# Attention heads whose transposed weights are spread over all 128 partitions by SBUF-to-SBUF transfers before their product with v

## The chip, the cores and the metric

The kernel runs on one core of a Trainium2 chip. Its engines are TensorE (PE, with its weight loads as PEld), VectorE (DVE), ScalarE (ACT), GpSimd (POOL), and SyncE (SP), whose queue issues all of this kernel's DMA transfers. The metric is the device time of one execution in microseconds. Span means the time from the first to the last instruction of the profiled execution.

## The reference

Two attention blocks over the same x (2048 tokens, 1024 wide, 32 heads of 32) are mixed by a gate per token. Block A is linear attention with a feature map phi, block B softmax attention:

```python
g = _sigmoid((x * gate_w).sum(-1, keepdims=True))
# A
pq, pk = phi(q), phi(k)
kv = jnp.einsum("bhsd,bhse->bhde", pk, v);  z = jnp.einsum("bhsd->bhd", pk)
o = jnp.einsum("bhqd,bhde->bhqe", pq, kv) / (jnp.einsum("bhqd,bhd->bhq", pq, z)[..., None] + 1e-6)
# B
scores = jnp.einsum("bhqd,bhkd->bhqk", q, k) * (Dh ** -0.5)
o = jnp.einsum("bhqk,bhkd->bhqd", softmax(scores), v)
# both: q, k, v are columns of x @ wqkv; o is brought to [2048, 1024] and multiplied by wo
return g * a + (1 - g) * b
```

All is float32. The kernel keeps that precision in its big products by splitting an operand into a high and a low part and adding three products (`three`).

## The kernel before

**Stages.** First, block B's v for the first 512 columns and all of its q and k are computed and stored to HBM (`v`, `qk`, and a second copy of v in another layout, `vh`). Then eight of B's heads (`NB = 8`) go one way (`bheads`), and the other 24 go another (`maxima` and `heads_`). The linear work of block A and the rest of v (`linear`, three matmuls L161 to L163 for each of eight k-steps, 512 columns each) fills TensorE beside both. The output projection comes last (`output`).

**The first eight heads.** They are worked on in 32 bursts, n = 4 h + J: head h and a quarter J of its 2048 query rows, that is four strips i of 128 queries. For each strip, four score matmuls (j, 512 keys each, L979) have 128 queries as rows. VectorE takes the maximum of each row in each block (L985, stored negated), ScalarE takes the exponential with that maximum as bias and the row sum beside it (L992, into a slot of `big20`), and VectorE transposes the 128 x 512 block in squares of 32 x 32 (L995, `move`). Since only squares are transposed, partition group a (32 partitions each) then holds, for its own 32 queries, keys m x 32 .. m x 32 + 31 of every square m. So in each group a key lies on 32 partitions only, and the product with v (`burst`, L865) is made of 32 x 32 x 128 matmuls: 16 squares m, four key blocks c, four groups a, 256 in a burst, with v copied to each of the four groups (`load_bv`, from `vh`). Four banks take the four groups' sums; the four key blocks c stand on different 32 rows of a bank, and each has been scaled by its own block maximum. ScalarE moves the four banks to `big2` (L871). At the end of a head `weigh` makes the factors that bring the four key blocks to a common maximum; `scale` multiplies by them (L936 to L942), `total` adds the four blocks (L954), and the result is stored to `oB` (L1089).

**Order.** The order of the instructions on each engine is fixed when the program is built. A planner keeps a clock for each of four engines (`T`, with `pe`, `act`, `dve`, `pool`), adds a cost for each piece of work (`AVB` for a burst, `EXPB`, `TRB`), and always takes what can start next; `tasks` go ahead of the streams. SP has no clock in it: its transfers stand in SP's queue in the order in which the planner comes to them, and each waits there for what it needs, with all others behind it. In `bheads` the scores of burst n wait until burst n - 2 is over, as the transposed blocks alternate between two sets of four tiles (`PT`).

**Memory.** `big0` to `big20` are tiles of 128 x 2048 float32, reused from stage to stage; `bank0` to `bank7` are the eight PSUM banks.

Of the kernel before, what the change touches and what calls it, by code (L numbers as in the profile page):

```python
# [9 lines left out]
F32 = mybir.dt.float32  # L10
# [32 lines left out]
NB = 8  # L43
EXPB, TRB, AVB, OEV = 0.68, 0.6, 4.3, 0.3
FEED = 2.4
# [3 lines left out]
def kernel(  # L49
# [50 lines left out]
    v_d = [dram.tile([P, NT, C], F32, name=f"v{c}") for c in range(NQC)]  # L100
    vh_d = dram.tile([C // DH, DH, S // DH, DH], F32, name="vh")
    wa_d = [[[dram.tile([HK, P, C], F32, name=f"wa{p}_{a}_{c}") for c in range(NQC)] for a in range(NK // HK)]
# [26 lines left out]
    def big_tile(i, dtype):  # L129
        return sb.tile([P, S], dtype, name=f"big{i}")  # L130

    big = [big_tile(i, F32R) for i in range(NBIG)]
    mid = [sb.tile([P, C], F32, name=f"mid{i}") for i in range(NMID)]
# [662 lines left out]
    p_free = [0.0] * NJ  # L796
    moved = [[] for _ in range(bn)]
    bursts = deque()
# [5 lines left out]
    def prepare():  # L804
        for i in PR + LACC + (SPARE, 14, 2):
            ft[i] = big_tile(i, F32)
# [12 lines left out]
        for i in (2, 3):  # L819
            nc.vector.tensor_add(fold, fold, ident[:, i * DH:(i + 1) * DH])  # L820
        ft["r"] = fr

    def load_bq(n):
# [5 lines left out]
        bq_ready[n] = T["pe"] + 5.0  # L829

    def load_bv(h):
        for a in range(4):
            nc.sync.dma_start(ft[14][a * DH:(a + 1) * DH, :], vh_d[h].rearrange("i b d -> i (b d)"))
        bv_ready[h] = T["pe"] + 8.0

    PT = ((6, 7, 8, 9), (10, 11, 15, 13))

    def place(n, j):

        return ft[PT[n % 2][j]].rearrange("p (m t q) -> p m t q", t=TPC, q=DH)  # L840

    def burst_at():
        if not bursts:
            return None
        n = bursts[0]
        h, J = divmod(n, NJ)
        if J == 0 and folded[0] < h - 1:
            return None
        return ended(moved[n], bv_ready[h])

    def burst_start():
        times = sorted(at for at in (ended(readers[b], free[b]) for b in RING if not held[b]) if at is not None)
        return both(burst_at(), times[3]) if len(times) > 3 else None

    def burst():
        n = bursts.popleft()
        h, J = divmod(n, NJ)
        bs = [take() for _ in range(4)]
        end = use("pe", AVB, *(free[b] for b in bs))
        v = ft[14].rearrange("p (b d) -> p b d", d=DH)  # L860
        for m in range(C // DH):
            for c in range(NJ):
                for a in range(4):
                    rows = slice(a * DH, (a + 1) * DH)
                    nc.tensor.matmul(bank[bs[a]][c * DH:(c + 1) * DH, :P], v[rows, c * (C // DH) + m, :],  # L865
                                     place(n, c)[rows, m], start=(m == 0), stop=(m == C // DH - 1))
        burst_end[n] = end
        ov = ft[2][:, J * C:(J + 1) * C].rearrange("p (t a q) -> p t a q", a=4, q=DH)
        for a in range(4):
            end = use("act", OEV, end)  # L870
            nc.scalar.copy(ov[:, :, a, :], bank[bs[a]][:, :P].rearrange("p (t q) -> p t q", q=DH))  # L871
            give(bs[a], end)
        if J == NJ - 1:
            if h + 1 < NB:
                load_bv(h + 1)
            folds.append((h, end))
        if kv_todo:
            keys_now(T["pe"])
# [4 lines left out]
    def weigh(h, at):  # L883
# [49 lines left out]
        def scale(J, ends):  # L933
# [6 lines left out]
            nc.scalar.copy(w, bank[b])  # L940
            o = ft[2][:, J * C:(J + 1) * C]
            nc.gpsimd.tensor_mul(o, o, w)  # L942
# [6 lines left out]
        def total():  # L949
            folds.popleft()  # L950
            b = take()
            end = use("pe", AV + AV_SWITCH, free[b])
            for j in range(NJ):
                nc.tensor.matmul(bank[b][j * DH:(j + 1) * DH, :], fold, ft[2][:, j * C:(j + 1) * C],  # L954
                                 start=True, stop=True)
# [6 lines left out]
        defer(first, at, 0.25, 1)  # L962

    def bheads():
        for i in range(NJ):
            load_bq(i)
        n_p = 0
        for n in range(bn):
            h, J = divmod(n, NJ)
            k = k_stack[h % 2]  # L970
            m = mx[h % 2].rearrange("p t j -> p (t j)")
            yield lambda: None if n > 1 and burst_end[n - 2] is None else 0.0
            for i in range(TPC):
                for j in range(NJ):
                    yield lambda: None if burst_at() is not None and burst_at() < T["pe"] else both(
                        bank_at(), bq_ready[n], *(k_ready[h] if n == 0 else ()))
                    b = take()
# [15 lines left out]

                    def move(_, n=n, i=i, j=j, src=src):
                        nc.vector.transpose(place(n, j)[:, :, i, :], src.rearrange("p (m q) -> p m q", q=DH))  # L995

                    item = defer(move, max(end, burst_end[n - 2] if n > 1 else 0.0), TRB, 0)
                    p_left[s] = [item]
                    moved[n].append(item)
            bursts.append(n)  # L1000
            tasks.append((burst_start, burst))
            if n + NJ < bn:
# [13 lines left out]
    def change():  # L1016
        q_stack[1], q_stack[2] = big_tile(2, F32R), big_tile(14, F32R)
        mid[2] = sb.tile([P, C], F32, name="mid2")
# [440 lines left out]
    advance("score")  # L1459
    load_bv(0)  # L1460
    for j in range(NJ):
        load_k(1, j)
# [80 lines left out]
```

## Time and profile before

| | |
|---|---|
| time, median of 2 runs | 3349.41 us (3346.39 to 3352.44) |
| profiled execution | 3338.3 us, span 3336.5 us, mean granted TensorE clock 0.97 |
| busy, share of the span | PE 92%, PEld 65%, DVE 66%, ACT 49%, POOL 44% |
| first to last matmul start of the bursts (L865) | 493.0 to 1497.1 us |
| DMA | 308603 packets, 410.66 MB, 123 GB/s over the span |

Times in the rows of the profile are microseconds unless marked ns. An instruction is named by engine, line of the kernel and tiles (what it writes <- what it reads, buffer numbers left out). A float32 matmul with float32 operands shows as two passes, so that L865's 8192 matmuls are 16384 entries and L1289's (the later heads' product) 1536 are 3072. Matmuls overlap: their pace is read from start to start. SPq rows are transfers that the SP queue issues: the duration is that of the issue, not of the transfer. A row of the timeline merges neighbours of one line (x12).

### The profile page before, as it was taken

To read this page: it belongs to the slowest core of one execution; us is meant where nothing else is said; L and a number is where in the kernel's file an instruction comes from. 1 tells how busy PE (TensorE), PEld (TensorE's weight loads), DVE (VectorE), ACT (ScalarE), POOL (GpSimd) and SP (SyncE) were. 2 spreads that over 40 slices of the span, in tenths; PEclk is the share of its full clock that TensorE was granted. 3 is DMA by queue.
4 is the path that set the end of the run, shared out by engine and by line. 5 is a ranking of instruction groups with operands and counts; after the bars stand their busy time and mean duration, and the time that the engine had idled before them with its cause. 6 is when DMAs were issued, how large, how long until landed. Compare 5 with 4: busy or idle time off the path is not lost.

```text
span 3336.5 us, 75056 instructions
## 1 busy us (share of the span) xinstructions
PE 3083.8 (92%) x30840; PEld 2174.2 (65%) x30840; DVE 2205.5 (66%) x3810; ACT 1618.8 (49%) x3528; POOL 1472.2 (44%) x528
## 2 busy tenths in 40 slices
PE   9999978888888888878999999999999999999999
PEld 8888866666676666666555555555556666666587
DVE  3222147575575665657888788888888888898622
ACT  3111125454454554533656566555656666566510
POOL 0000010110210201104789789889888888888100
PEclk9999999799989998899999999999999999999999
DMA  8885353432332433225323233223243344332442
GB/s 224 249 268 165 121 172 113 127 125 87 120 119 76 133 106 113 94 87 145 121 79 116 93 118 95 82 86 95 88 142 116 109 123 128 109 97 80 161 155 87
DMA packets 308603, 410.66 MB, mean 123 GB/s; under 512 B 110970, under 2 KB 187002, under 8 KB 304890
## 3 DMA queue, kind: packets, MB, share of 16 engines
q1 hardware_dynamic: 308260, 405.87, 39.2%
q8 instruction: 242, 3.96, 0.5%
q14 instruction: 101, 0.83, 0.1%
HBM read 291.77 MB, written 112.98 MB: 121 GB/s over the span
## 4 chain that ended last, share of the span: by engine, by line
PE 75%; DVE 13%; issue 6%; ACT 3%; DMA 2%; POOL 0%; SPq 0%; DVEq 0%; ACTq 0%
PE bank L161 13%; PE bank L163 12%; PE bank L162 12%; PE bank L1289 8%; PE bank L1193 8%; PE bank L865 8%; PE bank L1041 7%; DVE mx L1046 7%; PE bank L979 4%; ACT big L1197 2%; DVE bank L1105 1%; DVE bank L1251 1%; DVE mx L985 1%; DVE big L995 1%; DMA big<-xs 1%
## 5 line engine op out<-in xcount | busy, mean ns | idle before, releaser
L1242 POOL TENSOR_TENSOR big<-big,big 128x1792 f32<-128x1792 f32 (+1 forms) x322 | 1216.9, 3779 | 120.4 <-ACT big L1197 99.5
L1046 DVE TENSOR_REDUCE mx<-bank 128x1 f32<-128x512 f32 x1536 | 960.0, 680 | 153.0 <-PE bank L1041 151.7
L1197 ACT ACTIVATE big<-bank 128x512 f32<-128x512 f32 x1536 | 853.1, 608 | 373.7 <-PE bank L1193 332.4
L161 PE MATMUL bank<-big,big 128*128 128x512 f32 x2048 | 811.6, 396 | 25.5 <-DMA big<-xs 24.0
L163 PE MATMUL bank<-big,big 128*128 128x512 f32 x2048 | 805.1, 393 | 0.9 <-DVE big L268 0.4
L162 PE MATMUL bank<-big,big 128*128 128x512 f32 x2048 | 805.3, 393 | 0.0
L1041 PE MATMUL bank<-big,big 128*128 128x512 f32 x1536 | 610.3, 418 | 35.1 <-ACT big L1197 10.3
L1193 PE MATMUL bank<-big,big 128*128 128x512 f32 x1536 | 592.4, 406 | 16.8 <-DMA big<-ml 10.2
L161 PEld LDWEIGHTS bank<-big,big 128*128 128x128 f32 x2048 | 388.9, 190 | 116.9 <-issue 26.3
L163 PEld LDWEIGHTS bank<-big,big 128*128 128x128 f32 x2048 | 387.9, 189 | 86.4 <-DMA big<-xs 2.6
L162 PEld LDWEIGHTS bank<-big,big 128*128 128x128 f32 x2048 | 389.3, 190 | 80.1 <-issue 1.7
L985 DVE TENSOR_REDUCE mx<-bank 128x1 f32<-128x512 f32 x512 | 330.0, 668 | 144.9 <-PE bank L979 144.4
L865 PE MATMUL bank<-big,big 32*32 32x128 f32 x16384 | 272.0, 304 | 157.4 <-issue 153.9
L1041 PEld LDWEIGHTS bank<-big,big 128*128 128x128 f32 x1536 | 288.5, 189 | 196.6 <-DVE mx L1046 79.5
L992 ACT ACTIVATE big<-bank,mx 128x512 f32<-128x512 f32 x512 | 349.1, 688 | 131.4 <-DVE big L995 70.0
L1193 PEld LDWEIGHTS bank<-big,big 128*128 128x128 f32 x1536 | 284.2, 189 | 146.1 <-issue 44.1
L865 PEld LDWEIGHTS bank<-big,big 32*32 32x32 f32 x16384 | 216.1, 109 | 213.6 <-issue 186.4
L1289 PE MATMUL bank<-big,mid 128*32 128x512 f32 x3072 | 347.6, 597 | 0.0
L995 DVE STREAM_TRANSPOSE big<-big 128x512 f32<-128x512 f32 x512 | 340.1, 687 | 0.4 <-ACT big L992 0.2
L699 POOL TENSOR_TENSOR mid<-mid,mid 128x256 f32<-128x256 f32 x60 | 44.0, 733 | 453.9 <-DVE mid L694 430.7
L1289 PEld LDWEIGHTS bank<-big,mid 128*32 128x32 f32 x3072 | 96.2, 110 | 217.2 <-issue 216.9
L979 PE MATMUL bank<-big,big 128*128 128x512 f32 x512 | 209.5, 434 | 2.9 <-ACT big L871 0.9
(106 smaller groups left out, 1758.6 us busy)
## 6 DMA issues: line engine op xcount, KB each, us to landing
big<-xs SPq DMA_DIRECT2D x224, 512.0 KB
qk<-mid SPq DMA_DIRECT2D x128, 256.0 KB
big<-oA SPq DMA_DIRECT2D x64, 512.0 KB
big<-qk SPq DMA_DIRECT2D x480, 64.0 KB
big<-qk SPq DMA_DIRECT2D x72, 256.0 KB
xs<-big SPq DMA_DIRECT2D x64, 256.0 KB
oA<-mid SPq DMA_DIRECT2D x64, 256.0 KB
mid<-in_b_wqkv SPq DMA_DIRECT2D x48, 256.0 KB
```

Of the source, the lines that this page charges most:

```text
L161: yield nc.tensor.matmul(ps, sh, mh_, start=(kt == 0), stop=False)
L162: yield nc.tensor.matmul(ps, sh, ml_, start=False, stop=False)
L163: yield nc.tensor.matmul(ps, sl, mh_, start=False, stop=(kt == NK - 1))
L865: nc.tensor.matmul(bank[bs[a]][c * DH:(c + 1) * DH, :P], v[rows, c * (C // DH) + m, :], place(n, c)[rows, m], start=(m == 0), stop=(m == C ...
L985: nc.vector.tensor_reduce(m[:, col], bank[b], AX.X, ALU.max, negate=True)
L995: nc.vector.transpose(place(n, j)[:, :, i, :], src.rearrange("p (m q) -> p m q", q=DH))
L1041: nc.tensor.matmul(bank[b], q[:, t * P:(t + 1) * P], k[:, j * C:(j + 1) * C], start=True, stop=True)
L1046: nc.vector.tensor_reduce(m[:, t, j:j + 1], bank[b], AX.X, ALU.max)
L1193: nc.tensor.matmul(bank[b], k[:, t * P:(t + 1) * P], q[:, j * C:(j + 1) * C], start=True, stop=True)
L1197: nc.scalar.activation(pr_t[i][:, j * C:(j + 1) * C], bank[b], AF.Exp)
L1242: nc.gpsimd.tensor_add(lacc[:, :qp], lacc[:, :qp], pr(t)[:, :qp])
L1289: nc.tensor.matmul(av_b[j * DH:(j + 1) * DH, :], v[:, t, :], pr(t)[:, j * C:(j + 1) * C], start=(t == 0), stop=(t == NT - 1))
```

## The change

The heads, the scores, the maxima, the exponentials and the number and size of the transposes stay. The transposed squares no longer go to the place where the product reads them, but to one of three staging tiles (`STAGE`: `big9`, `big11`, `big15`), one for a strip, ordered by key block. From there `send` moves them with 16 transfers in a strip, SBUF to SBUF, 32 partitions x 512 columns each: the four groups a of 32 queries, times four quarters c of the squares. The destination is one tile `wide` of 128 x 8192 (in the place of `big6`, `big7`, `big8` and `big10`), in which quarter c lies on partitions 32 c to 32 c + 31 for all queries of the burst. So four squares of keys lie on 128 partitions beside each other, and the product (`burst`, now L885) is 16 matmuls of 128 rows and 512 columns: four steps m, four key blocks j, each of which is a column tile of 32 rows in one bank. ScalarE moves one bank instead of four.

A strip's transfers are taken up by the planner when its four transposes are done and the burst before is over (`send_at`); a burst needs all four strips sent (`sent`), and is planned 6 us behind the last. The scores of a strip wait until the staging tile's strip before has been sent (`gone`). v is read from `v` by `load_bv` with the keys on 128 partitions, for two heads by turns; `vh` and its stores are gone.

```diff
-EXPB, TRB, AVB, OEV = 0.68, 0.6, 4.3, 0.3
+EXPB, TRB, AVB = 0.66, 0.6, 3.5
+WIDE = (6, 7, 8, 10)
...
-        if c == 0:
-            for i in range(TPC):
-                nc.sync.dma_start(vh_d[:, :, t * TPC + i, :].rearrange("h i d -> i h d"),
-                                  va[i * DH:(i + 1) * DH, :].rearrange("p (h d) -> p h d", d=DH))
...
+    def bv_tile(h):
+        return ft[14][:, h % 2 * C:(h % 2 + 1) * C].rearrange("p (t d) -> p t d", d=DH)
+
     def load_bv(h):
+        c, o = divmod(h * DH, C)
+        nc.sync.dma_start(bv_tile(h), v_d[c][:, :, o:o + DH])
+        bv_ready[h] = T["pe"] + 6.0
...
+    STAGE = (9, 11, 15)
...
+    def send():
+        n, i, s, _ = sends.popleft()
+        dst = ft["wide"].rearrange("p (t a k) -> p t a k", a=4, k=C)
         for a in range(4):
-            nc.sync.dma_start(ft[14][a * DH:(a + 1) * DH, :], vh_d[h].rearrange("i b d -> i (b d)"))
-        bv_ready[h] = T["pe"] + 8.0
+            src = ft[STAGE[s]][a * DH:(a + 1) * DH, :].rearrange("p (c k) -> p c k", k=C)
+            for c in range(4):
+                nc.sync.dma_start(dst[c * DH:(c + 1) * DH, i, a, :], src[:, c, :])
+        there[n] = max(there[n], T["pe"] + 6.0)
+        sent[n] += 1
...
+    def send_at():
+
+        if not sends:
+            return None
+        n, i, s, items = sends[0]
+        return None if n and burst_end[n - 1] is None else ended(items)
...
     def burst():
         n = bursts.popleft()
         h, J = divmod(n, NJ)
-        bs = [take() for _ in range(4)]
-        end = use("pe", AVB, *(free[b] for b in bs))
-        v = ft[14].rearrange("p (b d) -> p b d", d=DH)
-        for m in range(C // DH):
-            for c in range(NJ):
-                for a in range(4):
-                    rows = slice(a * DH, (a + 1) * DH)
-                    nc.tensor.matmul(bank[bs[a]][c * DH:(c + 1) * DH, :P], v[rows, c * (C // DH) + m, :],
-                                     place(n, c)[rows, m], start=(m == 0), stop=(m == C // DH - 1))
+        b = take()
+        end = use("pe", AVB + AV_SWITCH, free[b])
+        v = bv_tile(h)
+        src = ft["wide"].rearrange("p (s m q) -> p s m q", m=NT, q=DH)
+        for m in range(NJ):
+            for j in range(NJ):
+                nc.tensor.matmul(bank[b][j * DH:(j + 1) * DH, :], v[:, j * NJ + m, :], src[:, :, j * NJ + m, :],
+                                 start=(m == 0), stop=(m == NJ - 1))
         burst_end[n] = end
...
             for i in range(TPC):
+                u = (n * TPC + i) % len(STAGE)
+                yield lambda: None if stage_left[u] and stage_left[u][0] not in gone else 0.0
...
+                sends.append((n, i, u, items))
+                tasks.append((send_at, lambda m=n * TPC + i: (send(), gone.add(m))))
             bursts.append(n)
-            tasks.append((burst_start, burst))
+            tasks.append((burst_at, burst))
```

In SP's queue before, the stretch in which one of the first bursts is worked on reads as follows: pairs of loads of x (`xs`, in two parts), a store of v, and the queries of a later burst.

```order
L490 DMA big4_220<-xs0_6_69 128x1024
L490 DMA big4_220<-xs1_6_85 128x1024
L327 DMA v1_161<-mid8_245 128x512
L828 DMA big0_216<-qk0_0_0_128 32x512 x2
L828 DMA big0_216<-qk0_1_0_136 32x512
L490 DMA big5_221<-xs0_7_70 128x1024
L490 DMA big5_221<-xs1_7_86 128x1024
L327 DMA v1_161<-mid9_246 128x512
```

The same stretch now, for the whole of the second burst (n = 1): its four strips leave `big11`, `big15`, `big9` and `big11`.

```order
L854 DMA wide_2847<-big11_2849 32x512 x16
L854 DMA wide_2847<-big15_2850 32x512 x16
L832 DMA big0_216<-qk0_0_0_128 32x512 x2
L832 DMA big0_216<-qk0_1_0_136 32x512
L854 DMA wide_2847<-big9_2848 32x512 x16
L491 DMA big5_221<-xs0_7_70 128x1024
L491 DMA big5_221<-xs1_7_86 128x1024
L332 DMA v1_161<-mid9_242 128x512
L854 DMA wide_2847<-big11_2849 32x512 x16
L491 DMA big4_220<-xs0_8_71 128x1024
L491 DMA big4_220<-xs1_8_87 128x1024
L332 DMA v1_161<-mid8_241 128x512
```

The other loads and stores stand where they stood, with 16 transfers of a strip two, one or none of them apart: 64 new entries of the queue for each burst.

On TensorE before, the first burst begins behind linear matmuls; here are its first rows (the banks of the four groups in turn, 256 rows in all).

```order
L163 MATMUL bank4_255<-big17_233,big4_220 128x512
L161 MATMUL bank4_255<-big18_234,big4_220 128x512
L865 MATMUL bank6_257<-big6_2915,big14_2925 32x128
L865 MATMUL bank7_258<-big6_2915,big14_2925 32x128
L865 MATMUL bank0_251<-big6_2915,big14_2925 32x128
L865 MATMUL bank2_253<-big6_2915,big14_2925 32x128
```

The second burst now is one row of 16, into one bank, with scores of the strips behind it (L1000, before L979).

```order
L168 MATMUL bank6_253<-big17_229,big5_221 128x512
L1000 MATMUL bank4_251<-big1_217,big0_216 128x512
L166 MATMUL bank6_253<-big17_229,big5_221 128x512
L885 MATMUL bank1_248<-wide_2847,big14_2854 32x512 x16
L1000 MATMUL bank3_250<-big1_217,big0_216 128x512
L1000 MATMUL bank5_252<-big1_217,big0_216 128x512
```

Between two bursts there stand 16 scores and 52 linear matmuls on average, nearly as many as before; 512 of the program's matmuls are bursts where 8192 were.

More of the change, by code (lines that the diff above doesn't have):

```diff
@@ L130, in big_tile, with wide_tile @@
         return sb.tile([P, S], dtype, name=f"big{i}")
-    big = [big_tile(i, F32R) for i in range(NBIG)]
+    def wide_tile(dtype):
+        return sb.tile([P, NJ * S], dtype, name="wide")
+    wide = wide_tile(F32R)
+    big = [wide[:, WIDE.index(i) * S:(WIDE.index(i) + 1) * S] if i in WIDE else big_tile(i, F32R)
+           for i in range(NBIG)]
     mid = [sb.tile([P, C], F32, name=f"mid{i}") for i in range(NMID)]
@@ L796 @@
     p_free = [0.0] * NJ
-    moved = [[] for _ in range(bn)]
     bursts = deque()
@@ L804, in prepare @@
     def prepare():
-        for i in PR + LACC + (SPARE, 14, 2):
-            ft[i] = big_tile(i, F32)
+        ft["wide"] = wide_tile(F32)
+        for n, i in enumerate(WIDE):
+            ft[i] = ft["wide"][:, n * S:(n + 1) * S]
+        for i in PR + LACC + (SPARE, 14):
+            if i not in WIDE:
+                ft[i] = big_tile(i, F32)
         raws[2:6] = [ft[SPARE][:, i * C:(i + 1) * C] for i in range(4)]
@@ L846, in burst_at @@
         h, J = divmod(n, NJ)
-        if J == 0 and folded[0] < h - 1:
+        if (J == 0 and folded[0] < h - 1) or sent[n] < TPC:
             return None
[L849 to L853, printed above, removed]
+        return both(there[n], bv_ready[h], bank_at())
     def burst():
@@ L857, in burst @@
         h, J = divmod(n, NJ)
[L858 to L872 removed]
+        b = take()
[6 more added lines that the diff above has]
+                                 start=(m == 0), stop=(m == NJ - 1))
+        burst_end[n] = end
+        end = use("act", 0.5, end)
+        nc.scalar.copy(ft[13][:, J * C:(J + 1) * C], bank[b])
+        give(b, end)
         if J == NJ - 1:
[L874 to L875 removed]
+            if h + 2 < NB:
+                load_bv(h + 2)
             folds.append((h, end))
@@ L953, in total @@
             for j in range(NJ):
-                nc.tensor.matmul(bank[b][j * DH:(j + 1) * DH, :], fold, ft[2][:, j * C:(j + 1) * C],
+                nc.tensor.matmul(bank[b][j * DH:(j + 1) * DH, :], fold, ft[13][:, j * C:(j + 1) * C],
                                  start=True, stop=True)
@@ L971, in bheads @@
             m = mx[h % 2].rearrange("p t j -> p (t j)")
-            yield lambda: None if n > 1 and burst_end[n - 2] is None else 0.0
             for i in range(TPC):
+                u = (n * TPC + i) % len(STAGE)
+                yield lambda: None if stage_left[u] and stage_left[u][0] not in gone else 0.0
+                items = []
                 for j in range(NJ):
-                    yield lambda: None if burst_at() is not None and burst_at() < T["pe"] else both(
-                        bank_at(), bq_ready[n], *(k_ready[h] if n == 0 else ()))
+                    yield lambda: both(bank_at(), bq_ready[n], *(k_ready[h] if n == 0 else ()))
                     b = take()
```

25 lines of the change are left out of this document (15 added, 10 removed).

## The prediction

> **What bounds the kernel now.** I read the page's first part, then the windows by stage, then the chain of waits inside the stage that the change touches, and last the timeline of TensorE and of the SP queue there.
>
> ```profile
> span 3336.5 us, 75056 instructions
> ...
> PE 3083.8 (92%) x30840; PEld 2174.2 (65%) x30840; DVE 2205.5 (66%) x3810; ACT 1618.8 (49%) x3528; POOL 1472.2 (44%) x528
> ```
> ```profile
> 0.00:458.00 458.00, 449.26 (x1963) 370.62 (x1963) 117.56 (x221) 93.44 (x163) 10.13 (x12) 0.99 0.67 201
> ...
> 1600.00:2600.00 1000.00, 956.06 (x4939) 566.70 (x4942) 838.26 (x1458) 596.45 (x1135) 866.64 (x226) 0.99 0.34 103
> ```
> ```profile
> 493.00:1497.00 1004.00, 837.84 (x19570) 658.34 (x19569) 629.94 (x1131) 501.57 (x1442) 125.09 (x142) 0.92 0.34 108
> ```
> Columns of the windows: length, then busy time of PE, weight load, DVE, ACT, POOL, then clock, DMA share, GB/s. TensorE is nearly full everywhere but in the third row, which spans the 32 bursts of the first eight heads: 838 of 1004 us, at clock 0.92. The chain of waits through that stage says why:
>
> ```profile
> by line: PE bank L865 24.8%; issue 15.4%; PE bank L161 12.0%; PE bank L162 11.7%; PE bank L163 11.6%; PE bank L979 11.4%; DVE mx L985 2.8%; DVE big L995 2.2%; PE bank L515 1.4%; DMA big<-xs 1.1%; POOL big L942 1.1%; PE bank L954 0.7%; PE ba
> ...
> 493.05 2.72 PE bank L865 x151
> ...
> 1485.30 2.12 PE bank L865 x115
> ```
> The bursts (L865) and the issue gaps inside them are 40% of it. First and last burst begin 992 us apart, 32.0 us for each of 31 periods. One burst, in the timeline of TensorE:
>
> ```profile
> 619.18 2.19 PE L865 MATMUL bank<-big,big 32*32 32x128 f32 x145
> 622.58 1.89 PE L865 MATMUL bank<-big,big 32*32 32x128 f32 x128 [1.22 <-issue]
> 626.58 2.27 PE L865 MATMUL bank<-big,big 32*32 32x128 f32 x128 [2.11 <-issue]
> 630.31 2.67 PE L865 MATMUL bank<-big,big 32*32 32x128 f32 x111 [1.46 <-issue]
> 632.91 1.65 PE L979 MATMUL bank<-big,big 128*128 128x512 f32 x3
> 634.36 0.50 PE L161 MATMUL bank<-big,big 128*128 128x512 f32 x1
> ```
> It holds TensorE from 619.18 to 632.91, 13.7 us, and leaves a slow clock: the three matmuls behind it take 1.45 us, 0.48 each, against the 0.23 from start to start in these rows:
>
> ```profile
> 601.05 0.39 PE L163 MATMUL bank<-big,big 128*128 128x512 f32 x1
> 601.28 0.39 PE L161 MATMUL bank<-big,big 128*128 128x512 f32 x1
> ```
>
> **The change part by part.** *The product.* 256 matmuls (512 passes in the trace) become 16 with 128 rows and 512 columns in four column tiles. The trace has exactly that work, four steps of the later heads' product:
>
> ```profile
> 1630.43 3.64 PE L1289 MATMUL bank<-big,mid 128*32 128x512 f32 x32
> 1634.00 0.66 PE L615 MATMUL bank<-ident,mid 128*128 128x128 f32 x4
> ```
> 32 passes, 3.6 us. So a burst gives TensorE back 10 us, 320 us over 32. If TensorE waits long ahead of a burst, the clock is slow again, as behind the old bursts, and the ends are 3.6 and twice that, 7.3 us; I take the middle, 5.5. The Trainium skill ("TensorE: Matmul & The Clock Gate", Part 1) has the half clock last for about 3.4 us of sustained work; by it the burst would be an estimated 5.3 us, and the half pitch above agrees with the half clock.
>
> *The transfers.* Each of the 128 strips (four a burst) is now sent by 16 transfers of 32 partitions x 2 KB: 64 in a burst, 2048 in all, all issued by SP. What SP needs for one:
>
> ```profile
> 455.11 5.53 SPq L828 DMA_DIRECT2D big<-qk  x12
> 460.73 1.76 SPq L833 DMA_DIRECT2D big<-vh  x4
> 462.53 7.43 SPq L776 DMA_DIRECT2D big<-qk  x12
> ```
> ```profile
> L828 SPq DMA_DIRECT2D big<-qk x96: 302/413/1691, 455.1 to 1347.2; - x96
> ```
> ```profile
> L1342 SPq DMA_DIRECT2D big<-mid x16: 507/513/590, 3165.1 to 3282.2; - x16
> ```
> ```profile
> 3182.52 0.38 SPq L1337 DMA_DIRECT2D big<-oB  x1
> 3182.95 0.51 SPq L1342 DMA_DIRECT2D big<-mid  x1
> 3183.56 1.01 SPq L1368 DMA_DIRECT2D out<-big  x2
> ```
> L828 has the same shape (32 partitions x 2 KB) from HBM: 12 from 455.11 to 460.64, the next at 460.73, so 5.62 / 12 = 0.47 each, its 0.41 and a gap of 0.05. L1342 is SBUF to SBUF with 32 partitions, in rows of 512 B: 0.51, never under 0.507; with the same gap 0.56, and 0.64 from its longest. The new ones have L828's shape and L1342's two ends. I take 0.56, because both ends lie in SBUF, and keep 0.47 and 0.64. SP alone then needs 2048 x 0.56 = 1147 us, and 963 us at 0.47, where the whole stage lasts 1004.
>
> It is worse than that sum, since the order is serial: one tile `wide` takes a burst's four strips, so the first transfer for burst n+1 waits for the last matmul of burst n, and burst n+1 waits for all 64 to land. The three staging tiles let VectorE run ahead, not SP. A period is therefore, one after the other:
> - 64 x 0.56 = 35.8 us of issue.
> - Other transfers that stand between strips in SP's queue: 313 in 32 bursts by the order of the changed kernel, 10 a period, at 0.36 (L490, below) to 0.41 with 0.05 gap: 4.3 us. Those between the last strip and the next first one (3 a period) hide in the two steps that follow.
> - Landing of the last: 2.3 us. The nearest row is the first query load, 2.0 us behind its issue; I add 0.3 for a loaded queue.
> - The burst, 5.5 us.
> - Stalls for slots, 1.0 us: in the built program a transfer waits for the one eight before it to land. The 12 loads of L776 above, beside the `vh` loads, took 7.43 where L828's took 5.53, 1.9 us lost. The `xs` pairs that stand between strips (about two a period) can do that; I take half of one.
>
> ```profile
> L490 SPq DMA_DIRECT2D big<-xs x224: 319/362/2607, 443.5 to 2404.9; - x112
> ```
> ```profile
> 455.57 2.01 DMA big<-qk
> ```
> Sum 48.9, say 49 us against 32.0. What else a period holds lies beside it: VectorE's 629.94 / 31 = 20 us (its transposes keep count and size; should the new write pattern double their 0.69 us it is 31 us, still hidden), ScalarE's 16 (one eviction for four), and TensorE's 52 linear matmuls and 16 scores, 68 x 0.23 = 16 us. So TensorE stands still about 25 us in each period, the gain of 10 us is spent there, and the linear work can't fill it: the planner, which costs a burst 3.85 us and knows no time of SP, puts about as much of it between bursts as before. Queued behind the waiting transfers on SP are query, key and `xs` loads, issued two units ahead; behind the waiting burst on TensorE stand the next scores and linear matmuls.
>
> *The rest.* The first burst: scores begin at 458 as before, strips come every 5.5 us, SP needs 9 us for each, so from about 466 the four take 36 us with 6 other transfers among them, and the burst begins near 510 and not 493: +17. Last burst 5.5 and not 12.4 us: -7. Twenty k-steps more of linear work (60 matmuls x 0.23) stand behind the last burst, six max scores fewer: +13. The 64 stores to `vh` vanish from the first stage; TensorE idles 458 - 449.26 = 8.7 us there, so they are worth 0 to 9, taken as 0. The loads of v by 128 B pieces replace as many `vh` loads, off the path.
>
> Sum: 31 x (49 - 32.0) + 17 - 7 + 13 = +550 us. The profiled execution took 3338.3 us (span 3336.5 and 1.8 around it), so it becomes 3888; the median of the two runs is 3349.4, 11 us above it, so **3900 us**.
>
> **The rivals.**
> - *SP issues at L828's price* (0.47): 30.1 + 4.3 + 2.3 + 5.5 + 1.0 = 43.2, +370 us, 3719. For it: the same shape. Against it: no SBUF-to-SBUF transfer of the trace goes under 0.507. 0.16. With a burst at full clock and no stalls it is 40.3 us a period, 3630.
> - *Landing decides*: when a transfer takes 6 us to land, as the `vh` loads (5.72 us in the chain below), eight slots give one every 0.75 us: 48 + 13 = 61 us, +920 us, 4270. Against it: 2.0 us for a 64 KB load. 0.08. It decides from 8 x 0.56 = 4.5 us on.
>
> ```profile
> 462.07 5.72 DMA big<-vh
> ```
> - *The other side: issue is cheap and only bytes count.* SP would have descriptors made for it ahead, at well under 0.3 us each, and the sends would run beside the other work. Then the DMA engines bound it: 4.2 MB more a period beside 108 GB/s x 32 us = 3.5 MB; at 268 GB/s, the best slice below, 28.7 us a period, 31 x (28.7 - 32.0) + 23 = -80 us, 3270. It decides where a period falls under 31.3 us, that is (31.3 - 13.1) / 64 = 0.28 us a transfer; the shortest issue in this stage is 302 ns, with its gap 0.35. 0.05. The Trainium skill ("DMA: Bandwidth & Descriptors", "Issuing engines are not separate DMA queues") calls the sequencer's time to start a transfer usually small relative to the transfer; by that rule this rival would hold, and the 0.51 us of L1342 against 2 us of landing, eight of them in flight, speaks against it.
>
> ```profile
> GB/s 224 249 268 165 121 172 113 127 125 87 120 119 76 133 106 113 94 87 145 121 79 116 93 118 95 82 86 95 88 142 116 109 123 128 109 97 80 161 155 87
> ```
> - *In between*, issue near 0.3 us: 3.0 us of slack either way, no change. 0.03.
>
> That the product isn't what it says can be left out: the built program has 16 matmuls in each burst.
>
> **How the numbers follow.** The forecast has 0.68, and its own range by issue 0.56 to 0.64, burst 3.6 to 7.3 and stalls 0 to 3 us is 46 to 58 us a period, 3810 to 4180. The range of 3650 to 4080 takes in most of that and most of the first rival; left out are landing (0.08), the faster side (0.05), no change (0.03) and a little at both ends. A measurement tells about 2% from no change here, 67 us. Faster 0.05, same 0.03, slower 0.92.
>
> **What would show it.** Right: the burst's 16 matmuls at 3.6 to 7 us each time, 45 to 57 us apart; SP's sends back to back at 0.5 to 0.64; TensorE's wait ahead of a burst ended by a transfer into `wide`; TensorE's busy share falling in the slices of that stage and its clock with it; the rest behind the last burst about as long as before (3336.5 - 1497.7, with 13 more some 1850 us). Wrong: sends under 0.35 us, gaps between the sends that a landing ends, or VectorE's transposes as what a strip waits for.

## The result, and the profile after

The changed kernel takes 4028.13 us (median of two runs, 4027.85 to 4028.41), against 3349.41 before: 1.203 times as long, with a 95% interval of 1.198 to 1.208. The forecast was 3900 us, in a range of 3650 to 4080, with 0.92 on slower.

The page after, its first part, the slices and the chain:

```profile
span 4026.1 us, 46866 instructions
...
PE 3059.5 (76%) x15480; PEld 2033.9 (51%) x15480; DVE 2222.3 (55%) x3810; ACT 1622.8 (40%) x3432; POOL 1472.2 (37%) x528
...
PE   9999754345454445454454999999999999999999
...
PEclk9999877677676677777676999999999999999999
...
PE 53%; SPq 25%; DMA 9%; DVE 7%; issue 3%; ACT 2%; POOL 0%; DVEq 0%; ACTq 0%; POOLq 0%
```

TensorE's busy share falls from 92% to 76%, though it has half as many instructions. In the slices where the bursts stand it is three to five tenths busy and its clock is about 0.7. A quarter of the chain that ended last is now SP's queue (SPq), which has 0% of the chain before.

The windows by stage, with the columns of the prediction: the time ahead of the bursts, the bursts, and the first 100 us behind the last one.

```profile
0.00:458.00 458.00, 447.98 (x1960) 369.95 (x1961) 117.26 (x221) 92.67 (x162) 10.13 (x12) 0.99 0.61 192
525.00:2211.00 1686.00, 800.92 (x4124) 501.88 (x4128) 640.18 (x1122) 497.94 (x1330) 123.86 (x141) 0.71 0.50 136
2211.70:2314.00 102.30, 100.27 (x579) 72.60 (x567) 92.70 (x164) 49.19 (x101) 58.32 (x28) 1.00 0.46 130
```

The stage of the bursts has grown from 1004 to 1686 us, and no engine in it is busy for half of that time. The two lines on which all hangs, the sends and the burst's matmuls, as groups (ns least/median/most, then the first and last start in us):

```profile
L854 SPq DMA_DIRECT2D wide<-big x2048: 507/589/1886, 474.2 to 2203.8; - x187
```
```profile
L885 PE MATMUL bank<-wide,big x1024: 589/1000/1062, 525.4 to 2211.2; 128*32 128x512 f32 x171
```

One period in the timeline of the SP queue, and the burst at each of its ends in the timeline of TensorE (start, length, and in brackets the idle time ahead and what ended it):

```profile
1023.71 20.36 SPq L854 DMA_DIRECT2D wide<-big  x32
1044.16 1.46 SPq L832 DMA_DIRECT2D big<-qk  x3
1045.73 0.84 SPq L491 DMA_DIRECT2D big<-xs  x2
1046.66 11.16 SPq L854 DMA_DIRECT2D wide<-big  x16
1057.92 1.03 SPq L491 DMA_DIRECT2D big<-xs  x2
1059.04 10.05 SPq L854 DMA_DIRECT2D wide<-big  x16
```
```profile
1017.78 5.86 PE L885 MATMUL bank<-wide,big 128*32 128x512 f32 x32 [11.12 <-DMA wide<-big]
1070.68 5.02 PE L885 MATMUL bank<-wide,big 128*32 128x512 f32 x32 [10.49 <-DMA wide<-big]
```

These eight rows hold a whole period. The burst ends at 1023.64, and the next send begins at 1023.71. The 64 sends take 20.36 + 11.16 + 10.05 = 41.6 us, the loads between them 3.8 us. The last send is issued at 1069.09, and the next burst starts 1.6 us later. With the burst's 5.9 us that is 52.9 us in which SP, the landing of the last send or the burst is at work at every moment, one after the other. First and last burst begin 1680.7 us apart (525.4 and 2206.1), so the mean is 54.2 us.

What TensorE waits for in that stage, from the list of waits (engine and line that wait, what they wait for, us in total, times, longest):

```profile
PE bank L166 <- DMA big<-xs: 412.0, 29, 26.1
PE bank L885 <- DMA wide<-big: 283.3, 28, 20.5
```

The bigger item isn't the burst but the linear work (L166): its `xs` loads stand in SP's queue behind the sends, so it comes late as well.

### The profile page after: what moved, and what is told of

It is laid out like the page before. It is cut to its first block, busy times and chain, and to the rows that moved or that the text cites. A ratio compares the mean times of both kernels' runs of the same rounds, so it can differ in the third digit from the quotient of the medians.

```text
span 4026.1 us, 46866 instructions
## 1 busy us (share of the span) xinstructions
PE 3059.5 (76%) x15480; PEld 2033.9 (51%) x15480; DVE 2222.3 (55%) x3810; ACT 1622.8 (40%) x3432; POOL 1472.2 (37%) x528
## 4 chain that ended last, share of the span: by engine, by line
PE 53%; SPq 25%; DMA 9%; DVE 7%; issue 3%; ACT 2%; POOL 0%; DVEq 0%; ACTq 0%; POOLq 0%
SPq L854 23%; PE bank L168 8%; PE bank L166 8%; PE bank L167 8%; PE bank L1219 8%; PE bank L1315 7%; PE bank L1067 7%; DMA big<-xs 5%; PE bank L885 4%; DVE mx L1072 4%; DMA wide<-big 2%; DMA v<-mid 1%; SPq L777 1%; PE bank L1000 1%; SPq L832 1%
## 5 line engine op out<-in xcount | busy, mean ns | idle before, releaser
L166 PE MATMUL bank<-big,big 128*128 128x512 f32 x1968 | 805.0, 409 | 489.5 <-DMA big<-xs 441.0
L168 PE MATMUL bank<-big,big 128*128 128x512 f32 x1936 | 786.0, 406 | 26.3 <-DMA big<-xs 25.6
L167 PE MATMUL bank<-big,big 128*128 128x512 f32 x1840 | 744.5, 405 | 0.4 <-POOL big L479 0.4
L1268 POOL TENSOR_TENSOR big<-big,wide 128x1792 f32<-128x1792 f32 (+1 forms) x184 | 695.7, 3781 | 79.7 <-ACT wide L1223 59.9
L1017 DVE STREAM_TRANSPOSE big<-big 128x512 f32<-128x512 f32 x512 | 344.8, 692 | 618.8 <-DMA wide<-big 583.9
L166 PEld LDWEIGHTS bank<-big,big 128*128 128x128 f32 x1968 | 386.3, 196 | 585.8 <-issue 333.3
L1067 PE MATMUL bank<-big,big 128*128 128x512 f32 x1536 | 612.7, 416 | 29.8 <-DVE mx L1072 8.4
L1219 PE MATMUL bank<-big,big 128*128 128x512 f32 x1536 | 593.7, 405 | 5.7 <-DVE mid L1134 0.8
L1223 ACT ACTIVATE wide<-bank 128x512 f32<-128x512 f32 x884 | 496.6, 607 | 220.0 <-PE bank L1219 201.6
L1268 POOL TENSOR_TENSOR big<-big,big 128x1792 f32<-128x1792 f32 (+1 forms) x138 | 521.7, 3780 | 41.9 <-ACT big L1223 30.1
L168 PEld LDWEIGHTS bank<-big,big 128*128 128x128 f32 x1936 | 377.7, 195 | 133.8 <-DMA big<-xs 51.7
L1223 ACT ACTIVATE big<-bank 128x512 f32<-128x512 f32 x652 | 369.5, 605 | 166.0 <-PE bank L1219 149.7
L885 PE MATMUL bank<-wide,big 128*32 128x512 f32 x1024 | 175.9, 849 | 331.7 <-DMA wide<-big 283.3
L167 PEld LDWEIGHTS bank<-big,big 128*128 128x128 f32 x1840 | 362.4, 197 | 76.2 <-POOL big L479 1.6
L1067 PEld LDWEIGHTS bank<-big,big 128*128 128x128 f32 x1536 | 288.2, 188 | 185.0 <-DVE mx L1072 78.0
L1219 PEld LDWEIGHTS bank<-big,big 128*128 128x128 f32 x1536 | 284.1, 188 | 136.6 <-issue 38.6
L885 PEld LDWEIGHTS bank<-wide,big 128*32 128x32 f32 x1024 | 44.7, 149 | 451.1 <-issue 446.2
L1000 PE MATMUL bank<-big,big 128*128 128x512 f32 x512 | 204.2, 440 | 61.6 <-ACT big L1013 53.4
```

Of the source, the lines that this page charges most:

```text
L166: yield nc.tensor.matmul(ps, sh, mh_, start=(kt == 0), stop=False)
L167: yield nc.tensor.matmul(ps, sh, ml_, start=False, stop=False)
L168: yield nc.tensor.matmul(ps, sl, mh_, start=False, stop=(kt == NK - 1))
L885: nc.tensor.matmul(bank[b][j * DH:(j + 1) * DH, :], v[:, j * NJ + m, :], src[:, :, j * NJ + m, :], start=(m == 0), stop=(m == NJ - 1))
L1017: nc.vector.transpose(dst[:, j * NJ:(j + 1) * NJ], src.rearrange("p (m c q) -> p m c q", c=4, q=DH))
L1067: nc.tensor.matmul(bank[b], q[:, t * P:(t + 1) * P], k[:, j * C:(j + 1) * C], start=True, stop=True)
```

## The experiments

The kernel before took 3339 to 3345 us beside these runs (a single run, or the median of seven beside `ringpoolhalf` and `diag`). Each version ran once, `diag` four times. A period is the time from the start of the first burst's first matmul to that of the last one's, through 31.

**What sets the price of a send.** Two theories on the 0.59 us: the two ends in SBUF, or the shape and number of the transfers. `hbmsrc` leaves SBUF as the source: the sends read rows of the same shape from HBM, so the transposed weights never reach the product, and no send waits for a transpose.

```diff
-                nc.sync.dma_start(dst[c * DH:(c + 1) * DH, i, a, :], src[:, c, :])
+                nc.sync.dma_start(dst[c * DH:(c + 1) * DH, i, a, :], qk_d[1][0][n // 4][a * DH:(a + 1) * DH, c * C:(c + 1) * C])
```


> The 2048 transfers keep their shape, number, destination and bytes, but read 32 rows x 2 KB of the stored keys in HBM instead of the staging tile (so the product gets wrong operands, and a transfer no longer waits for the transposes). Measured with the change: 0.633 us from one transfer of a strip to the next, a period of 54.2 us. Theory, SP's issue sets the period: the issue falls to the 0.47 us of such loads, the period to 54.2 - 64 x 0.163 = 43.8 us, the time to 4028 - 31 x 10.4, near 3705 us. Rival, bytes or landing set it: the same bytes through the same engines, now with a read of HBM, so 54 us or more and 4028 or more.

3711.58 us, a period of (1884.5 - 518.3) / 31 = 44.1 us, as expected. The group of the sends, and one period in SP's timeline:

```profile
L854 SPq DMA_DIRECT2D wide<-qk x2048: 302/419/1804, 475.5 to 1882.2; - x187
```
```profile
1012.92 17.11 SPq L854 DMA_DIRECT2D wide<-qk  x32
1030.13 1.29 SPq L832 DMA_DIRECT2D big<-qk  x3
1031.46 7.38 SPq L854 DMA_DIRECT2D wide<-qk  x16
```

The same 64 KB, the same number of partitions, the same destination: 0.419 and not 0.589 us each, so the source in SBUF costs 0.17 us a transfer, and 64 x 0.17 = 10.9 us a period explains the 10 us gained. The transposes, for which these sends no longer wait, aren't where it comes from: SP's waits for them in the changed kernel are a few us in all (shown further down). The theory holds; that the price comes from shape or number falls, and so does the rival of the expectation, that bytes or landing set the period.

`halfbytes` keeps the number and sends half the columns (256 of 512), the rest of `wide` being a constant.

```diff
-                nc.sync.dma_start(dst[c * DH:(c + 1) * DH, i, a, :], src[:, c, :])
+                nc.sync.dma_start(dst[c * DH:(c + 1) * DH, i, a, :C // 2], src[:, c, :C // 2])
```


> Each of the 2048 transfers carries 256 of its 512 columns (1 KB rows), the other halves of the wide tile keep a constant; the product gets wrong operands. Theory, the number of issues sets the period: nothing changes, 54 us a period, 4010 to 4030 us. Rival, bytes or landing: the 40 us that a burst's transfers take come down towards 20, the period to 34 to 45 us, 3400 to 3750 us.

4021.38 us, as expected: half the bytes of the sends are worth 7 us of 4028. Their group reads as before:

```profile
L856 SPq DMA_DIRECT2D wide<-big x2048: 507/589/1914, 475.8 to 2187.7; - x187
```

So in the changed kernel the bytes of a send count for next to nothing. How many of them SP has to issue is tried further down, in `act` and `pool`.

**What the product alone is worth.** `nosend` has no transfers into `wide` (it holds a constant); scores, exponentials, transposes and the new product stay.

```diff
-                nc.sync.dma_start(dst[c * DH:(c + 1) * DH, i, a, :], src[:, c, :])
+                pass
```


> All 2048 transfers are left out, the product reads a constant tile; order of all else unchanged. It is what the new product would give if spreading the blocks cost nothing. Theory (only the transfers cost): a period is set by VectorE (20 us busy) or TensorE (16 us of scores and linear work and a burst of 3.6 at full clock, 20.5), 21 to 24 us, so 4028 - 31 x 31, some 3030 to 3100 us, faster than before. Rival, the order or the staging itself holds the stage: a period of 32 us or more, 3340 or more.

2995.05 us, 350 us below the kernel before, a period of 21.7 us. The first part and the clock of its page, and the burst's group:

```profile
PE 2905.1 (97%) x15480; PEld 1976.0 (66%) x15480; DVE 2204.7 (74%) x3810; ACT 1614.1 (54%) x3432; POOL 1480.1 (49%) x532
...
PEclk9999998999999999999999999999999999999999
```
```profile
L887 PE MATMUL bank<-wide,big x1024: 592/592/617, 500.1 to 1175.0; 128*32 128x512 f32 x171
```

The period is as expected; the time is 35 us below the 3030 to 3100 expected. 31 x (54.2 - 21.7) takes 4028 to 3020, and the first burst begins at 500.1 and not at 525.4, which the expectation left out.

The product is as good as read from the later heads: 32 passes in 3.64 us, every time, at full clock. The gain that the change could bring is there, (32.0 - 21.7) x 31 = 320 us of it in the bursts' stage. The transfers cost 4028 - 2995 = 1033 us and eat it three times over. The linear work is in time as well: TensorE's waits of L166 for `xs` loads in the bursts' stage are 10.4 us here, where they were 412.0.

**What is serial, and what is SP's.** The prediction had two causes for the period: SP's issue, and that the first send waits for the burst before. `ring` takes away only the second: `wide` gets a fifth place, and the first strip of a burst is sent while the burst before it still waits or runs. Where a burst's strips wrap around the ring, its product is made in two ranges of columns (64 passes). The result of the heads moves to `big2` and four small buffers to `big13`.

```diff
-WIDE = (6, 7, 8, 10)
+WIDE = (6, 7, 8, 10, 12)
...
+        slot_ = (n * TPC + i) % len(WIDE)
...
-        return None if n and burst_end[n - 1] is None else ended(items)
+        back = n - 1 if i else n - 2
+        return None if back >= 0 and burst_end[back] is None else ended(items)
```


> The wide tile gets a fifth place, and the strips take the five places in turn; so the first strip of a burst can be sent while the burst before still waits or runs (the product of a burst whose places wrap is cut into two column ranges; the weights' loading buffers move to another tile for this stage). The number and size of transfers stay. Theory, issue in a serial order: landing and burst (1.7 + 5.5 us) are hidden behind the first strip's issue, the period falls from 54.2 to 47, SP never stands still, 4028 - 31 x 7.2, near 3805 us. Rival, the serial order costs nothing beside the issue (slots or landings hold SP anyway): 53 to 54 us, 4000 to 4030.

3892.35 us, a period of (2065.5 - 525.6) / 31 = 49.7 us, between the two expectations. The 2065.5 is the start of the last burst's second range, which needs the strips sent last; its first range begins at 2053.0, and counted by that the period would be 49.3. Of the 7.2 us that landing and burst take (1.7 + 5.5), 4.5 are gained and not the whole. SP's timeline shows where the rest is:

```profile
559.88 1.02 SPq L491 DMA_DIRECT2D big<-xs  x2
560.99 0.38 SPq L332 DMA_DIRECT2D v<-mid  x1
561.46 10.59 SPq L854 DMA_DIRECT2D wide<-big  x16
572.16 1.03 SPq L491 DMA_DIRECT2D big<-xs  x2
573.27 0.38 SPq L332 DMA_DIRECT2D v<-mid  x1
573.75 21.60 SPq L854 DMA_DIRECT2D wide<-big  x32
```

Each row begins within 0.12 us of the end of the one ahead: SP's queue never pauses in this stretch. All its rows added up, between the first and the last burst and for each of 31 periods, say where the other 2.7 us are. In the changed kernel SP issues sends for 37.8 us, other transfers for 5.8, has 3.9 of small gaps (to 0.2 us each) and stands still for 6.5; in `ring` it is 38.3, 5.8, 4.0 and 1.7. So the pause was 6.5 us and not 7.2, since some `xs` loads were issued in it; 1.7 of waiting is left, and the sends take 0.4 more. The serial step was real, but it is an eighth of the period, and SP's own work with its gaps, 47.5 us, is nearly all the rest.

**Who issues.** `act` lets ScalarE's queue issue the sends of odd groups a, 32 of 64.

```diff
-                nc.sync.dma_start(dst[c * DH:(c + 1) * DH, i, a, :], src[:, c, :])
+                (nc.scalar if a % 2 else nc.sync).dma_start(dst[c * DH:(c + 1) * DH, i, a, :], src[:, c, :])
```


> The transfers of two of the four query groups (8 of 16 in a strip) are issued by ScalarE's queue, the others by SP. Theory, issue by one queue: SP's part is 32 x 0.633 = 20.3 us, the period 34 us if ScalarE keeps up; it has 16 us of work and now 20 us of issue, so 34 to 38 us, 3400 to 3530 us. Rival, one descriptor generator or the DMA engines behind both queues: 54 us, 4028.

3624.13 us, a period of 41.5: 404 us better than the changed kernel, and 94 us above the top of what was expected. ScalarE's timeline shows the miss, and behind it the group of its sends with who waited for any of the sends:

```profile
1009.93 10.16 ACTq L854 DMA_DIRECT2D wide<-big  x16
1020.14 0.69 ACT L1013 ACTIVATE big<-bank,mx 128x512 f32<-128x512 f32 x1 [9.63 <-DMA wide<-big]
```
```profile
L854 ACTq DMA_DIRECT2D wide<-big x1024: 513/602/1792, 478.9 to 1784.6; - x171
...
who waited for it (us, times):
  ACT big L1013: 455.6, 69
```

ScalarE is no spare queue. While it issues 16 sends, 10.16 us, it makes no exponential, and the exponentials wait 455.6 us for sends. The transposes behind them are late in turn: in the bursts' stage VectorE waits 387.2 us for exponentials, where it was 9.0 in the changed kernel, and with the transposes a burst's later strips are late. The theory that two queues halve the issue is right as far as it goes, and left out whose work stands behind the issue.

`pool` gives the same 32 sends to GpSimd, which has little to do in this stage (123.86 of 1686 us above, 7% and not the 14% of the expectation).

```diff
-                nc.sync.dma_start(dst[c * DH:(c + 1) * DH, i, a, :], src[:, c, :])
+                (nc.gpsimd if a % 2 else nc.sync).dma_start(dst[c * DH:(c + 1) * DH, i, a, :], src[:, c, :])
```


> The transfers of two of the four query groups (8 of 16 in a strip) are issued by GpSimd, which is 14% busy in this stage, and not by ScalarE, whose exponentials waited behind its issues (41.5 us a period, 3624 us). Theory: SP's part is 20.3 us, the period 20.3 + 13.7 = 34 us if GpSimd needs no more than SP for one, 3400 us; no trace here shows a transfer that GpSimd issues, so the upper end is where 1 us for each makes 32 + 7 us and more, 39 to 42, 3560 to 3650. Rival, one generator behind all queues: 54 us.

3462.27 us, a period of 36.2, 2 us above the 34 of the theory. The groups of the two queues:

```profile
L854 POOL DMA_DIRECT2D wide<-big x1024: 496/498/662, 468.5 to 1620.3; - x171
L854 SPq DMA_DIRECT2D wide<-big x1024: 507/589/1505, 474.4 to 1631.9; - x171
```

GpSimd issues one in 0.50 us, so it is no dearer than SP, and the period falls by 18 us of the 20.3 that 32 sends at 0.633 would take off.

**Both, and the next limit.** `ringpool` is `ring` with the issue of `pool`.

```diff
-                nc.sync.dma_start(dst[c * DH:(c + 1) * DH, i, a, :], src[:, c, :])
+                (nc.gpsimd if a % 2 else nc.sync).dma_start(dst[c * DH:(c + 1) * DH, slot_, a, :], src[:, c, :])
```


> Both of it: five places and half of the transfers issued by GpSimd. Theory: SP issues 32 x 0.633 + 13 others x 0.45 = 26 us a period and hides landing and burst, so 26 to 28 us if GpSimd keeps up, 4028 - 31 x 27, near 3190 us, faster than both kernels; at 1 us for each of GpSimd's 32, 32 to 34 us and 3340 to 3400. Rival, landing or bytes decide once issue is cheap (4.2 MB and 3.5 MB a period at 268 GB/s, 28.7 us): 3240.

3351.78 us, a period of (1522.4 - 510.4) / 31 = 32.6. That is where the kernel before stands. The time falls into what was expected for 1 us a send on GpSimd, but by luck: GpSimd issues at 0.50 us here too. The window of its stage:

```profile
510.00:1380.00 870.00, 638.47 (x4030) 433.76 (x4031) 551.95 (x971) 428.17 (x1153) 512.76 (x961) 0.85 0.83 225
```

The 16 DMA engines are now 83% busy at 225 GB/s, where the changed kernel had 50% at 136. `ringpoolhalf` asks whether that is the limit: `ringpool` with 256 of 512 columns sent.

```diff
-                (nc.gpsimd if a % 2 else nc.sync).dma_start(dst[c * DH:(c + 1) * DH, slot_, a, :], src[:, c, :])
+                (nc.gpsimd if a % 2 else nc.sync).dma_start(dst[c * DH:(c + 1) * DH, slot_, a, :C // 2], src[:, c, :C // 2])
```


> Five places and half of the transfers by GpSimd, with 256 of the 512 columns in each transfer (the other halves of the wide tile keep a constant, the product gets wrong operands). With all columns: 32.7 us a period, DMA engines busy 0.83 of the stage at 225 GB/s, 3352 us. Theory, with the issue divided among two queues bytes decide: 2.1 MB a period less, so 26 to 28 us (SP's own 26), 3352 - 31 x 6, near 3170. Rival, still the issue (SP's and GpSimd's together): 32 to 33 us, 3340 to 3360.

3267.92 us, a period of (1438.7 - 507.6) / 31 = 30.0, between the two expectations:

```profile
510.00:1330.00 820.00, 635.70 (x4137) 432.95 (x4129) 559.94 (x987) 436.36 (x1172) 531.12 (x985) 0.87 0.60 175
```

Bytes are part of it, for here they do gain 84 us, where the same cut in `halfbytes` gained 7. The larger part is SP's queue again. Its rows added up as for `ring`, for each of 31 periods: in `ringpool` it issues sends for 19.8 us and other transfers for 6.0, has 2.4 of small gaps and stands still for 4.5; in `ringpoolhalf` it is 19.5, 5.9, 2.5 and 2.2. So SP's own work is 28 us in both, 2 us above the 26 that was worked out, and what the bytes change is how long it stands still. More than half of that is sends that wait for a load of x to land, in SP's list of waits in `ringpool` (525 to 1400 us):

```profile
SPq L854 <- DMA big<-xs: 75.4, 64, 3.0
```

In `ringpoolhalf` the same wait is 30.5 us in 40 places, in the changed kernel, over its whole stage, 20.0 in 25. GpSimd issues for 15.8 us a period and is 59% busy in the window of `ringpool` above. That the 30.0 us are still 8 above the period of `nosend` is SP's work too: 27.9 us of them.

**A version that beats both.** A quarter of the sends (a = c) move nothing to other partitions. `diag` is `ringpool` with these as plain copies, by GpSimd and ScalarE in turn; 48 transfers a burst are left.

```diff
+                to = dst[c * DH:(c + 1) * DH, slot_, a, :]
+                if a == c and a % 2:
+                    nc.gpsimd.tensor_copy(to, src[:, c, :])
+                elif a == c:
+                    use("act", 0.6)
+                    nc.scalar.copy(to, src[:, c, :])
+                else:
+                    (nc.gpsimd if a % 2 else nc.sync).dma_start(to, src[:, c, :])
```


> Five places, half of the transfers by GpSimd, and the four blocks of a strip that stay on their partitions (a = c) copied by ScalarE (two) and GpSimd (two) and not sent; 48 transfers in a burst. Theory, bytes decide: 1.05 MB a period less, 6.4 of 7.4 MB, so 28 to 29 us a period and 3352 - 31 x 4, near 3230, 3% faster than before. GpSimd then has 24 x 0.5 + 8 x 1.3 + 4 = 26 us a period, ScalarE 16 + 5. Rival, the copies hold up ScalarE's queue as its own transfers did (41.5 us a period with half of the transfers on it): no gain over 3352, or slower.

3226.32 us (four runs, 3214.47 to 3237.92) beside 3345.17 for the kernel before: 0.964 times, 95% interval 0.960 to 0.968, and a period of (1405.5 - 509.4) / 31 = 28.9 us, all as expected. Its page and the window of its stage:

```profile
PE 2975.5 (92%) x16088; PEld 2021.8 (63%) x16088; DVE 2214.2 (69%) x3810; ACT 1758.7 (54%) x3688; POOL 1997.7 (62%) x1552
```
```profile
510.00:1350.00 840.00, 669.91 (x4422) 456.66 (x4414) 598.02 (x1061) 599.16 (x1504) 593.94 (x1062) 0.89 0.80 220
```

The DMA engines are about as full as in `ringpool`, 0.80, and the period is a ninth shorter. The copies take a quarter off the bytes of the sends and off the number that SP and GpSimd issue (SP's own work falls from 28 to 23 us a period), so this run doesn't tell the two apart, and what holds the period at 28.9 stays open.

## Why the prediction was right, and where it missed

The outcome was right, and for the reason given: the likeliest case, not a rival, is what happened. The sum was 128 us too low.

- **The mechanism** held step by step. Landing of a transfer into `wide` ends TensorE's wait ahead of a burst, the sends begin right behind the burst's end (0.06 us behind it in the median of 31), and VectorE's transposes aren't what a strip waits for. It is the other way round: VectorE is idle for 618.8 us ahead of the transposes, and 583.9 of them end with a send, which frees the staging tile (first row below). The transposes didn't get dearer by their new write pattern either, 692 ns against 687 before. Gaps between the sends that a landing ends, a sign of being wrong, are there but small: 20.0 us in the whole stage (second row, from SP's list of waits). SP's waits for transposes are 3.7 us (third row):

```profile
L1017 DVE STREAM_TRANSPOSE big<-big 128x512 f32<-128x512 f32 x512 | 344.8, 692 | 618.8 <-DMA wide<-big 583.9
```
```profile
SPq L854 <- DMA big<-xs: 20.0, 25, 2.6
SPq L854 <- DVE big L1017: 3.7, 10, 0.5
```

- **The price of a send is the term that was mis-sized**: 0.56 us taken, 0.633 measured. The row of L1342, 507/513/590, was read by its median, but nearly all its transfers stood behind one of another line or a pause, not behind one of their own. In the changed kernel's timeline of SP, the first of the 32 sends from 1023.71 shown above, by itself:

```profile
1023.71 0.51 SPq L854 DMA_DIRECT2D wide<-big  x1
```

  The first takes 0.513 and costs 0.56 with its gap, just as predicted. Those right behind it take 0.589, with a gap of 0.044 between them: 20.36 / 32 = 0.636. The one transfer of L1342 that stood right behind another is its longest, the 0.590, the second of these three in SP's timeline of the kernel before, 0.04 us behind the first (the third, 0.10 us behind, took 0.535):

```profile
3168.42 1.77 SPq L1342 DMA_DIRECT2D big<-mid  x3
```

  The prediction had that value, 0.64, as the upper end; a strip of 16 should have been priced by it. 64 x 0.073 = 4.7 us a period, 31 of them 145 us, is the whole miss and a little more; the smaller ones below nearly cancel, and the 11 us that the forecast added for the median did not come (4028.13 in the median, 4027.85 profiled). L828 shows the same two prices in the kernel before, 302 least and 413 median.
- **Others and stalls**: 4.3 + 1.0 predicted. 54.2 - 40.5 (64 x 0.633) - 5.5 - 1.7 leaves 6.5. The other transfers alone are 5.8 us of issue, 411 in 31 periods at 0.44, dearer than the 0.36 to 0.41 taken. The stalls for slots, 20.0 / 31 = 0.6, were taken at 1.0.
- **Landing**: 2.3 predicted, 1.5 to 1.9 measured. **Burst**: 5.5 predicted, 5.50 the mean of 32, from 3.64 to 6.34. The middle of two ends was right because most bursts begin at the slow clock: 30 of the 32 take 4.9 us or more, and two the 3.64 of the full clock. The Trainium skill ("TensorE: Matmul & The Clock Gate", Part 1) has the slow clock last some 3.4 us of sustained work; the estimate of 5.3 us by it agrees with the 5.50.
- **First burst**: +17 predicted, +32 measured (525.4 against 493.0): the first send starts at 474.2 and not 466, and the sends of four strips take 44.7 and not 36 us, 49.6 with the loads between them.
- **Behind the last burst**: +13 predicted, and -25 measured (from the last burst's end, 1839 us before and 1814 after). The sign was wrong. Counting the linear steps left over was not enough. The same time in two runs with the changed kernel's order, from the burst's last matmul to the end of the span, is 1820 in `hbmsrc` and 1818 in `nosend`, however long the sends took, so it is the new order of the work and not something that TensorE caught up on. Right behind the last burst the kernel before has this:

```profile
1497.70:1600.00 102.30, 88.49 (x480) 63.63 (x480) 81.24 (x143) 39.91 (x85) 49.34 (x29) 0.93 0.45 130
```

  TensorE is busy for 88.5 us of it at clock 0.93, and for 100.3 us at 1.00 after. Which instruction of the order brings that wasn't tried apart.
- The sum as it came: 31 x (54.2 - 32.0) = 688, + 32 - 7 (last burst) - 25 = +688 us, against 4026.1 - 3336.5 = 689.6.

Of the rivals, *only bytes count* falls by `halfbytes` in the kernel as it was changed: at 0.59 us of issue by one queue SP can't fill the DMA engines, which are half busy. It comes back in part once two queues issue and the serial step is gone: half the bytes are then worth 2.6 us a period (`ringpoolhalf`), beside 28 us of SP's own work. The Trainium skill's rule that stood against the forecast ("DMA: Bandwidth & Descriptors", "Issuing engines are not separate DMA queues": issuing from several engines saves the initiation only, usually small beside the transfer) is right in its first half and was misleading in its second: the initiation was 41.6 of a period of 52.9 us, and issuing half of it elsewhere was worth 566 us in `pool`. *Landing decides* falls by the 1.6 us between last send and burst; the 5.72 us of its condition was that of a load of 256 KB, four times a send. *SP at L828's price* is just what `hbmsrc` shows: 44 us a period where 43.2 was worked out, 3712 where 3719 was; its condition, a source in HBM, was not the kernel's.

## What to carry to other kernels

Price a new row of transfers by how many stand behind one another on their queue: take the issue time of neighbours that go back to back, with their ends in the same two memories, times their number, and put it beside the time of the stage before looking at a byte. When a queue is full, look for an issuer that has nothing else to do; an engine that computes pays for every transfer it issues with its own work, and the work behind it. And when the issue is spread over two queues, add up each queue again before blaming the DMA engines: here they were 0.83 busy, and SP's own work was still 28 of 32.6 us. Sending only what really has to change its partitions takes load off both.

## What was not expected of the hardware

- The issue time of a 64 KB transfer of 32 partitions depends on where it starts and what stands ahead of it, not on its bytes: on SP, with both ends in SBUF, 0.513 us for the first of a row of sends and 0.589 for each right behind it, against 0.419 in the median and 0.302 at least with the source in HBM, and 0.589 again with half the bytes. On ScalarE it is 0.60, on GpSimd 0.498 in the median and never under 0.496.
- A loaded SP queue delays what isn't in question: of TensorE's waits in the stage, 412.0 us were for `xs` loads queued behind the sends, 283.3 for the sends themselves.
- With two queues issuing, the 16 DMA engines are 0.83 busy at 225 GB/s in the mix of loads, stores and SBUF-to-SBUF transfers, and the wait of SP's sends for loads of x to land grows from 20.0 to 75.4 us.
